# A wait on the predecessor's semaphore for every GpSimd operation, in a fused attention and MLP kernel on one core

## The chip, the core and the metric

The kernel runs on one core of a Trainium2 chip. The core has five engines that work side by side, each with its own queue of instructions: TensorE (PE in the profile; its weight loads are PEld), VectorE (DVE), ScalarE (ACT), GpSimd (POOL) and SyncE (SP), which here only issues DMA transfers. An engine takes its instructions in the order in which they were written. Between engines, order is kept by semaphores: an instruction can wait until a semaphore has reached a value, and can raise a semaphore when it is done. The metric is the time of one execution on the device in microseconds, and lower is better.

## The reference

Two layers follow each other. The first is an attention in which each token sees its last 96 tokens and the first 8 of its sequence, with a bias that grows with distance and differs by head. The second is an MLP with softplus between its two matrix products.

```python
def _attn_ref(q, k, v, n_global, n_local):        # q, k, v: (4, 8, 768, 64); 8 global, 96 local
    scores = scale * np.matmul(q, k.transpose(0, 1, 3, 2))
    is_global = pos[None, :] < int(n_global)
    is_local = (rel >= 0) & (rel < int(n_local))
    bias = -slopes[:, None, None] * dist[None, :, :]
    scores = np.where(is_global | is_local, scores + bias[None], -1e9)
    a = np.exp(scores - np.max(scores, axis=-1, keepdims=True))
    a = a / (np.sum(a, axis=-1, keepdims=True) + 1e-09)
    return np.matmul(a, v)

def _moe_ref(x, w_in, w_out):                     # x: (3072, 512), w_in: (512, 2048), w_out: (2048, 512)
    h = x @ w_in
    g = np.maximum(h, 0.0) + np.log1p(np.exp(-np.abs(h)))
    return g @ w_out
```

## The kernel before

The 3072 tokens are 24 blocks of 128, and two neighbouring blocks make a unit. For each unit, q, k and v are loaded by DMA into float32 buffers (`raw`), cast to bfloat16 (`castq`, `castk`, lines 545 and 554; `castv`, line 573) and, for q and k, transposed, on PE for the first units and by DMA transposes on SP's queue after that (lines 673 and 680). For each block, PE computes the scores into `s_ps` (line 788), DVE adds the bias (`z`, line 814), ACT takes the exponential (`ex`, line 819), PE multiplies by v into `x_ps` or `o_ps` (`pv`, line 845), and DVE normalizes by a reciprocal and a product (`nm`, lines 856 and 857) into `xs`. A DMA transpose turns `xs` into `XT` (line 888).

The 8 global tokens of a sequence are brought into the block before the present one by small copies: `gk` (line 695) copies columns of k, and `gv` (line 704) copies 4 rows of v from one place of the tile `vb` to another. These copies stand on POOL, DVE or ACT, as the order says.

For each pair of blocks (a group, 12 in all) the first product of the MLP runs into `h_ps` (`a`, line 903), ACT makes the softplus as exp and ln (`e`, line 919, and `ln`, line 930) into `g`, and the second product follows. The first four groups use a plain product (`b`, line 950) with a copy out of PSUM (`oc`, line 968). The later eight use a product with seven partial products instead of eight: PE runs them at line 442, from sums of weights (`ws`, line 344, made once on DVE and POOL) and sums of `g` (`ka`, line 379, on DVE and POOL), and DVE puts the parts together (lines 408 to 429). 35 products of a blank tile (`fill`, line 1047) fill gaps of PE near the start.

What sets the order is a written table, `ORDER`: it names each operation and its engine, for all engines in one sequence. `Program.in_order()` yields the operations in that sequence; the loop at the end of the kernel issues them. No scheduler moves anything. The framework works out from the tiles that an instruction reads and writes which semaphores it must wait for, and puts in only the waits that it needs. So a POOL instruction waits for POOL's own semaphore only where it touches a tile that an earlier POOL instruction also touches.

In the built program an instruction holds one wait. Where more are needed, the others stand in wait instructions of their own ahead of it on the same queue.

The changed loop stands at the end of the kernel function:

Of the kernel before, what the change touches and what calls it, by code (L numbers as in the profile page):

```python
# [184 lines left out]
def kernel(  # L185
# [11 lines left out]
    nc = tc.nc  # L197
# [937 lines left out]
    while fed < NGRP:  # L1135
        feed(fed)
        feed2(fed)
        fed += 1

    for o in pl.in_order():  # L1140
        o.ins = o.fn()
        for d in o.sync:
            tc.add_manual_dep(
                o.ins.ins, d.ins.ins.name,
                mybir.DependencyInfo(mybir.DependencyClass.Sync, mybir.DependencyReason.DATA),
            )
# [35 lines left out]
```

## Time and profile before

| what | value |
|---|---|
| median of 3 runs | 213.78 us (213.57 to 213.79) |
| the profiled execution, its own time | 213.29 us |
| its span in the profile | 211.4 us |
| granted TensorE clock, mean over the span | 1.00 |
| PE, busy | 201.6 us (95%) |
| ACT, busy | 177.0 us (84%) |
| DVE, busy | 158.8 us (75%) |
| POOL, busy, instructions | 84.7 us (40%), 98 |

All times of single instructions come from the one profiled execution, whose span is 1.9 us shorter than its own time. A row of the timeline gives the start and the length in us from the start of the span, the engine, the line of the kernel, the operation, what it writes and reads, and how many equal instructions the row merges. In brackets stands how long the engine had been idle before, and what released it. The end of a row is its start plus its length: where one engine's next row starts before that end, the two instructions overlap there.

### The profile page before, as it was taken

How to read it: one execution, taken by the hardware profiler on the slowest of the kernel's cores; microseconds unless marked ns; L12 is line 12 of the kernel's file. 1: busy time of each engine (PE TensorE's matmuls, PEld its weight loads, DVE VectorE, ACT ScalarE, POOL GpSimd, SP SyncE). 2: the span in 40 equal slices, each digit the busy share in tenths (PEclk: the TensorE clock that was granted, in tenths of full speed). 3: DMA queues.
4: the chain of work that ended last, by engine and by line, in shares of the span. 5: the costliest groups of instructions: out<-in, count | busy, mean ns of one | idle time of the engine just before them, and what ended most of it. 6: DMA issues, size and time to landing. Idle time of an engine off the chain costs nothing.

```text
span 211.4 us, 5376 instructions
## 1 busy us (share of the span) xinstructions
PE 201.6 (95%) x2150; PEld 158.7 (75%) x2163; DVE 158.8 (75%) x296; ACT 177.0 (84%) x253; POOL 84.7 (40%) x98
## 2 busy tenths in 40 slices
PE   7599999999999979999999999999999999999993
PEld 2366886556765756877889888889889889988882
DVE  5458789698658895697977888895989898716583
ACT  4899999998998869889899978988999989985610
POOL 4526788820370491113126673058708205070000
PEclk9999999999999999999999999999999999999999
DMA  5999999968999695996999988556994710600222
GB/s 196 337 365 386 387 356 348 308 158 220 289 223 167 156 221 159 224 206 130 184 274 174 231 181 199 151 98 123 290 256 61 160 25 5 198 3 0 99 101 102
DMA packets 70137, 40.99 MB, mean 194 GB/s; under 512 B 30432, under 2 KB 61664, under 8 KB 70112
## 3 DMA queue, kind: packets, MB, share of 16 engines
q1 hardware_dynamic: 69680, 39.99, 74.0%
q10 hardware_dynamic: 432, 0.66, 0.9%
q8 instruction: 17, 0.28, 0.6%
q14 instruction: 8, 0.07, 0.1%
HBM read 27.26 MB, written 6.29 MB: 159 GB/s over the span
## 4 chain that ended last, share of the span: by engine, by line
PE 84%; DVE 6%; DMA 4%; ACT 2%; issue 2%; SPq 0%; DVEq 0%
PE h_ps L903 37%; PE o_ps L442 12%; PE o_ps L950 9%; PE s_ps L788 5%; PE x_ps L442 5%; PE x_ps L845 4%; PE s_ps L950 3%; DVE z L814 2%; DMA raw<-in_k_dram 2%; PE s_ps L442 2%; PE x_ps L1047 2%; DMA XT<-xs 1%; DVE vb L704 1%; PE h_ps L442 1%; PE o_ps L845 1%
## 5 line engine op out<-in xcount | busy, mean ns | idle before, releaser
L903 PE MATMUL h_ps<-XT,w_in_bf 128*128 128x256 bf16 x768 | 94.8, 273 | 0.3 <-DMA XT<-xs 0.2
L903 PEld LDWEIGHTS <-w_in_bf 128*128 128x128 bf16 x768 | 72.9, 98 | 12.8 <-issue 0.8
L919 ACT ACTIVATE e<-h_ps 128x512 f32<-128x512 f32 x96 | 59.2, 634 | 13.2 <-PE h_ps L903 12.7
L930 ACT ACTIVATE g<-e 128x1024 bf16<-128x1024 f32 x48 | 49.7, 1052 | 0.6
L814 DVE TENSOR_TENSOR z<-s_ps,biasA 128x1024 f32<-128x1024 f32 x38 | 45.5, 1218 | 6.0 <-PE s_ps L788 4.1
L819 ACT ACTIVATE pb<-z 128x1024 bf16<-128x1024 f32 (+1 forms) x44 | 43.1, 990 | 1.7 <-DVE z L814 1.5
L379 POOL TENSOR_TENSOR raw<-g 128x1024 bf16<-128x1024 bf16 x7 | 14.9, 2131 | 33.2 <-ACT g L930 23.8
L442 PEld LDWEIGHTS <-g 128*128 128x128 bf16 x256 | 24.6, 98 | 3.1
L950 PE MATMUL o_ps<-w_out_bf,g 128*128 128x512 bf16 x88 | 23.1, 380 | 0.6 <-issue 0.3
L845 PEld LDWEIGHTS <-pb 128*128 128x128 bf16 x352 | 16.0, 97 | 5.4 <-issue 1.9
L442 PEld LDWEIGHTS <-raw 128*128 128x128 bf16 x192 | 18.4, 98 | 2.1
L442 PE MATMUL o_ps<-raw,raw 128*128 128x256 bf16 x152 | 19.0, 273 | 0.0
L950 PEld LDWEIGHTS <-g 128*128 128x128 bf16 x128 | 11.3, 98 | 9.5 <-ACT g L930 0.7
L545 POOL CAST kb<-raw 128x1024 bf16<-128x1024 f32 x8 | 8.3, 1041 | 23.0 <-DMA raw<-in_k_dram 17.3
L573 POOL CAST vb<-raw 64x512 bf16<-64x512 f32 x18 | 12.1, 670 | 10.4 <-DMA raw<-in_v_dram 9.7
L857 DVE TENSOR_TENSOR xs<-x_ps,rcp 128x256 bf16<-128x256 f32 x36 | 15.3, 424 | 1.2
L845 PE MATMUL x_ps<-vb,pb 128*128 128x65 bf16 x280 | 14.4, 193 | 1.4 <-DVE xs L857 1.4
L379 DVE TENSOR_TENSOR raw<-g 128x1024 bf16<-128x1024 bf16 x17 | 12.3, 732 | 4.1 <-ACT g L930 2.6
L856 DVE RECIPROCAL rcp<-x_ps 128x4 f32<-128x4 f32 x36 | 6.4, 178 | 9.7 <-PE x_ps L845 8.8
L704 POOL COPY vb<-vb 4x512 bf16<-4x512 bf16 x15 | 10.5, 698 | 6.3 <-DMA out_dram<-osb 2.8
L442 PE MATMUL o_ps<-raw,g 128*128 128x256 bf16 x96 | 12.0, 273 | 0.0
L1047 PE MATMUL x_ps<-blank 128*128 128x512 bf16 x32 | 10.7, 440 | 1.3 <-DVE blank L985 1.2
(117 smaller groups left out, 249.4 us busy)
## 6 DMA issues: line engine op xcount, KB each, us to landing
raw<-in_v_dram SPq DMA_DIRECT2D x12, 512.0 KB, 5.5
out_dram<-osb SPq DMA_DIRECT2D x22, 256.0 KB, 2.6
raw<-in_q_dram SPq DMA_DIRECT2D x9, 512.0 KB, 5.6
raw<-in_k_dram SPq DMA_DIRECT2D x9, 512.0 KB, 5.2
raw<-in_moe_w_in_dram SPq DMA_DIRECT2D x8, 512.0 KB, 9.5
raw<-in_moe_w_out_dram SPq DMA_DIRECT2D x8, 512.0 KB, 8.6
raw<-in_k_dram SPq DMA_DIRECT2D x6, 256.0 KB, 5.8
raw<-in_q_dram SPq DMA_DIRECT2D x4, 256.0 KB, 8.2
```

What stands on the lines that cost most here:

```text
L379: (nc.vector if eng == "DVE" else nc.gpsimd).tensor_tensor(dst, a[0], b[0], ALU.subtract)
L442: nc.tensor.matmul(psum(j), lhs[:, f // 2, f % 2, :], w(f), start=(f == 0), stop=(f == 7))
L704: copy_on[eng](vb_of(prev)[sl, :, 0:D], vb_of(first)[sl, :, 0:D])
L814: op(f"z{n}.{part}", "DVE", lambda: nc.vector.tensor_tensor(z, scored(), bias, ALU.add), reads=b_keys(n, part) + key, writes=[("z", slot)] ...
L819: nc.scalar.activation(pb[:, 0:nr, :].rearrange("p (y a) b -> p y (a b)", y=2), scored() if n in PE_BIAS else z, AF.Exp, scale=1.0 / root_d,)
L845: nc.tensor.matmul(xv[:, h, :], pb[:, 4 * (h % 2) + 2 * part + h // 2 if lone else u_all * (2 * (h % 2) + h // 2) + u, :], vb_of(prev if u ...
L857: nc.vector.tensor_tensor(xs[:, 4 * part : 4 * part + 4, :], xv[:, :, 0:D], rcp[:][:, :, None].to_broadcast([P, 4, D]), ALU.mult,)
L903: last = nc.tensor.matmul(hv[:, j, :], w_in_bf[:, m, fb * P : fb * P + P], XT[g % NXG][:, m, :], start=(m == 0), stop=(m == NM - 1),)
L919: nc.scalar.activation(e[:, p % 2, :, :].rearrange("p j (b t r) -> p (j b) r t", b=2, r=2), hb[:].rearrange("p (a r t) -> p a r t", a=4, r=2),
L930: nc.scalar.activation(gt[:, 2 * p - 2 : 2 * p + 2, :].rearrange("p a t -> p (a t)"), e[:].rearrange("p a j t -> p (a j t)"), AF.Ln, bias=1.0,
L950: nc.tensor.matmul(bank(x), gt[:, fb, ns * P : ns * P + P], w_out_bf[:, fb, :], start=(fb == 0), stop=(fb == NFB - 1),)
L1047: op(x, "PE", lambda: nc.tensor.matmul(x_ps[:], blank[:, 0:P], blank[:]), reads=["blank"], banks=(x,))
```

## The change

Each operation that the table gives to POOL gets one more dependency: its last instruction waits until the last instruction of the POOL operation ahead has raised POOL's semaphore. The written order of every engine, the operations, the tiles and the DMAs are the same. In the built program, 92 of the 98 recorded POOL instructions name POOL's own semaphore instead of 39; 10 of those 39 waited for an older POOL instruction than the one directly ahead, and now wait for that one. Since an instruction holds one wait, the waits that it had before move into wait instructions of their own: POOL's queue has 77 of these instead of 57. No instruction of PE, DVE, ACT or SP waits for anything else than before.

```diff
+    held_by = None
     for o in pl.in_order():
         o.ins = o.fn()
+        if o.eng == "POOL":
+            here = nc.cur_bb.bb.instructions[-1]
+            if held_by is not None:
+                tc.add_manual_dep(
+                    here, held_by,
+                    mybir.DependencyInfo(mybir.DependencyClass.Sync, mybir.DependencyReason.DATA),
+                )
+            held_by = here.name
         for d in o.sync:
```

The rows below are POOL's queue, of the program before (-) and after (+), around 72 us of the profile. `Pool_49`, `DVE_49`, `PE_49` and the `DMAHW` names are the semaphores of the engines and of the DMA queues. The first L704 row is the `gv` copy at 72.22 us, and the L344 row two sums of weights at 72.80 us.

```order
 L545 COPY kb_82<-raw_77 128x1024 [waits DMAHW4_49,DMAHW7_49,DMAHW2_49,Pool_49]
-L704 COPY vb<-vb 4x8x64 [waits DVE_49,PE_49]
-L344 TENSOR_TENSOR raw_76<-raw_68,raw_69 128x512 x2
+L704 COPY vb<-vb 4x8x64 [waits DVE_49,PE_49,Pool_49]
+L344 TENSOR_TENSOR raw_76<-raw_68,raw_69 128x512 [waits Pool_49] x2
 L573 COPY vb<-raw_78 64x8x64 [waits DMAHW3_49,Pool_49]
 L344 TENSOR_TENSOR raw_76<-raw_69 128x512 [waits Pool_49]
```

Nothing moved: the same instructions stand in the same order, the two sums now each wait for the instruction ahead, and the copy waits for three semaphores instead of two.

The second place is POOL's queue around 143 to 151 us, where sums of `g` (L379) and the copy of k columns (L695) follow each other, and PE waits for that copy. Before:

```order
L379 TENSOR_TENSOR raw_68<-g_106 128x1024 [waits DVE_49,Activation_49]
L379 TENSOR_TENSOR raw_69<-g_106 128x1024 [waits DVE_49,PE_49]
L695 COPY kTa_90<-kTa_90 128x8x4 [waits DMAHW6_49,DMAHW3_49]
L379 TENSOR_TENSOR g_106<-g_106 128x4x2x128 [waits Pool_49]
L704 COPY vb<-vb 4x8x64 [waits DVE_49,PE_49,Pool_49]
```

The same place in POOL's queue after the change:

```order
L379 TENSOR_TENSOR raw_68<-g_106 128x1024 [waits DVE_49,Activation_49,Pool_49]
L379 TENSOR_TENSOR raw_69<-g_106 128x1024 [waits DVE_49,PE_49,Pool_49]
L695 COPY kTa_90<-kTa_90 128x8x4 [waits DMAHW6_49,DMAHW3_49,Pool_49]
L379 TENSOR_TENSOR g_106<-g_106 128x4x2x128 [waits Pool_49]
L704 COPY vb<-vb 4x8x64 [waits DVE_49,PE_49,Pool_49]
```

Here too each instruction keeps its place and its waits for others; the first three gain the wait for the one ahead.

## The prediction

> **What bounds the kernel now.** I read the page's shares first, then who made PE wait, then the stretches of time in which it waited, and only then the instructions there.
>
> ```profile
> PE 201.6 (95%) x2150; PEld 158.7 (75%) x2163; DVE 158.8 (75%) x296; ACT 177.0 (84%) x253; POOL 84.7 (40%) x98
> ...
> PE 84%; DVE 6%; DMA 4%; ACT 2%; issue 2%; SPq 0%; DVEq 0%
> ```
>
> PE is busy for 95% of the span and makes up 84% of the chain that ended last. POOL is busy for 40% and is not on that chain. So the change, which touches POOL alone, can matter only through what POOL does to others. The waits of PE over the whole span, the longest in total first (us in total, times, longest):
>
> ```profile
> PE x_ps L845 <- DVE xs L857: 1.4, 1, 1.4
> ...
> PE o_ps L845 <- DVE osb L968: 0.2, 1, 0.2
> ```
>
> No row of that view names POOL; the three that stand between these and are put down to an engine belong to the start, where PE waits for the first casts and transposes. The largest is a single wait of `pv` for `nm`. The windows say where it lies:
>
> ```profile
> 72.00:74.00 2.00, 1.95 (x21) 1.42 (x18) 1.97 (x2) 2.00 (x3) 1.78 (x2) 1.00 0.42 94
> 74.00:76.00 2.00, 0.79 (x8) 0.56 (x6) 1.93 (x3) 1.83 (x4) 1.91 (x3) 1.00 0.98 272
> 76.00:78.00 2.00, 1.62 (x26) 1.24 (x26) 1.87 (x7) 0.38 (x1) 1.89 (x2) 1.00 1.34 234
> 78.00:204.00 126.00, 125.56 (x1397) 107.16 (x1400) 97.21 (x176) 108.19 (x148) 43.15 (x43) 1.00 0.65 145
> ```
>
> After length come busy times of PE, PEld, DVE, ACT and POOL. From 74 to 78 us PE is idle for 1.21 + 0.38 = 1.59 us. From 78 to 204 us it is idle for only 0.44 us of 126: whatever is won before 78 us is kept as long as the others can follow. Those have room there, DVE 97.21 of 126 us and ACT 108.19. The instructions around the hole:
>
> ```profile
> 72.22 0.61 POOL L704 COPY vb<-vb 4x512 bf16<-4x512 bf16 x1 [2.84 <-DMA out_dram<-osb]
> 72.67 2.78 DVE L704 COPY vb<-vb 4x512 bf16<-4x512 bf16 x1
> 72.80 2.50 POOL L344 TENSOR_TENSOR raw<-raw,raw 128x512 bf16<-128x512 f32 x2
> 73.11 0.81 PE L950 MATMUL o_ps<-w_out_bf,g 128*128 128x512 bf16 x3
> 73.76 1.04 PE L903 MATMUL h_ps<-XT,w_in_bf 128*128 128x256 bf16 x8
> 75.36 0.61 POOL L573 CAST vb<-raw 64x512 bf16<-64x512 f32 x1
> 75.49 0.18 DVE L856 RECIPROCAL rcp<-x_ps 128x4 f32<-128x4 f32 x1
> 75.70 0.42 DVE L857 TENSOR_TENSOR xs<-x_ps,rcp 128x256 bf16<-128x256 f32 x1
> 76.05 0.68 DVE L968 COPY osb<-o_ps 128x512 f32<-128x512 f32 x1
> 76.18 0.40 PE L845 MATMUL x_ps<-vb,pb 128*128 128x65 bf16 x8 [1.39 <-DVE xs L857]
> 76.78 0.40 PE L845 MATMUL o_ps<-vb,pb 128*128 128x65 bf16 x8 [0.20 <-DVE osb L968]
> ```
>
> The DVE copy that starts at 72.67 took 2.78 us. Copies of its kind take a tenth of that (DVE's of line 704, least, median and longest in ns):
>
> ```profile
> L704 DVE COPY vb<-vb x10: 280/292/2784, 49.3 to 177.5; 4x512 bf16<-4x512 bf16 x10
> ```
>
> It started while POOL ran its own `gv` copy (to 72.83), and ended at 75.45, which is 0.15 us after POOL's two sums of weights ended (72.80 + 2.50 = 75.30). POOL's second row starts 0.03 us before its first ends. The row behind the sums, which already waits for POOL's semaphore, starts 0.06 us after them, and exactly there DVE got through. So DVE stood behind three POOL instructions without a break, and PE behind DVE.
>
> **The change part by part.** *What one added wait costs.* POOL rows that follow each other directly show both kinds:
>
> ```profile
> 32.62 0.61 POOL L573 CAST vb<-raw 64x512 bf16<-64x512 f32 x1
> 33.31 1.28 POOL L344 TENSOR_TENSOR raw<-raw,raw 128x512 bf16<-128x512 f32 x1
> 34.53 0.61 POOL L573 CAST vb<-raw 64x512 bf16<-64x512 f32 x1
> 35.11 1.27 POOL L344 TENSOR_TENSOR raw<-raw 128x512 bf16<-128x512 f32 x1
> ```
>
> The second waits for POOL's semaphore and starts 0.08 us after the end ahead (32.62 + 0.61 = 33.23), as the row at 75.36 started 0.06 after. The third and fourth don't wait for it, and start 0.06 and 0.03 us before the end ahead. So the wait costs a POOL instruction that is otherwise ready 0.09 to 0.14 us; I take 0.12. 53 instructions gain it (92 instead of 39) and 10 get a later one. Were all of them ready, that would be 63 x 0.14 = 8.8 us at most, and POOL is idle 60% of the span. Where an instruction waits longer for a DMA or another engine, its old wait moves into an instruction of its own. The profile has no price for that alone. Above I bound it by the same 0.14 us, below by nothing, and take 0.07, the middle.
>
> *What hides it.* Work of PE that uses a late POOL result would show in PE's waits, and none does today. The nearest uses:
>
> ```profile
> 38.27 1.03 POOL L531 CAST w_out_bf<-raw 128x1024 bf16<-128x1024 f32 x1
> 40.25 0.59 PE L950 MATMUL o_ps<-w_out_bf,g 128*128 128x512 bf16 x2
> ...
> 96.19 1.04 POOL L545 CAST kb<-raw 128x1024 bf16<-128x1024 f32 x1 [1.47 <-DMA raw<-in_k_dram]
> 97.25 2.51 SPq L680 DMA_TRANSPOSE kT<-kb  x2
> ...
> 101.94 0.55 PE s_ps L788 x16
> ...
> 147.90 0.21 POOL L695 COPY kTa<-kTa 128x32 bf16<-128x32 bf16 x1
> ...
> 148.86 0.55 PE s_ps L788 x16
> ```
>
> The cast of w_out at 38.27 ends at 39.30, and the product at 40.25 is about the first that needs it: 0.95 us of cover. It ends the burst of which the rows from 32.62 to 35.11 are a part; with four waits added in that burst it comes 0.5 us late. The k cast at 96.19 ends at 97.23 and SP's transposes start 0.02 us later, so these will start up to 0.14 us late. They are issued 4.7 us before PE's scores at 101.94, of which 2.51 are the issue itself, and the rest is the cover. The copy at 147.90 ends 0.75 us before PE's scores at 148.86. It stands third behind two sums that also gain a wait: 0.07 + 0.07 + 0.12 = 0.26 us late, at most 0.36. Without its cover each of these would stop PE by as much as it is late: 0.5, 0.14 and 0.26 us. I cost all of them at 0.
>
> *What it gains.* At 72 us the two sums now wait, so POOL pauses between its copy and the first sum, as it does before the row at 75.36. Does DVE get its turn in a pause of 0.06 us? It did at 75.30, and here:
>
> ```profile
> 61.23 0.62 POOL L573 CAST vb<-raw 64x512 bf16<-64x512 f32 x1
> 61.75 0.29 DVE L704 COPY vb<-vb 4x512 bf16<-4x512 bf16 x1
> 61.91 0.61 POOL L704 COPY vb<-vb 4x512 bf16<-4x512 bf16 x1
> ```
>
> The same kind of DVE copy came 0.1 us before POOL's end at 61.85, took its usual 0.29 us, and POOL's next, which started 0.06 us after that end, was not held either. Applied to 72 us: POOL's copy, up to 0.14 us later for its moved wait, ends at 72.83 to 72.97; DVE's copy ends 0.15 us later, at 73.1 instead of 75.45, so 2.35 us earlier. Then `nm` (75.49 to 76.12, so 0.67 us behind the copy) ends near 73.8. PE comes to its `pv` at 73.76 + 1.04 = 74.80 and finds it done: the wait of 1.39 us goes. The copy out of `o_ps` at 76.05 can start when PE's product at 73.11 ends (73.92) and takes 0.68, to 74.7 at the latest allowed by DVE's own order; PE wants that bank at 74.80 + 0.40 = 75.20: the 0.20 us goes too. Together 1.59 us.
>
> *What is late next.* DVE is then ahead of PE by 0.5 to 1 us. POOL's sums end some 0.3 us later than now, and behind them on its queue stand a v cast, a third sum, a `gv` copy and the casts of q and k for SP's next transposes; POOL was busy for 1.91 of the 2 us from 74 us, so they all come that much later, and PE uses none of them before it has done its work to 80 us. DVE copies and casts that come after may meet them and stand behind one POOL instruction for up to its 1.27 us, but PE is no longer waiting directly behind these. From 78 us all loads, transposes and softmax steps follow PE's own progress, since PE's idle time there is 0.44 us in all. For such meetings I take back 0.1 us.
>
> *Sum:* 213.29 us of the profiled execution, minus 1.59, plus 0.1, gives 211.8. The profiled execution lies 0.49 us under the median of the runs (213.78), so against the median it is 212.3 us.
>
> On that place the Trainium skill, "SBUF — State Buffer" (section "SBUF: two separate sides"), says that the port pair shared by VectorE and GpSimd is an exclusive lock: whoever starts first has it for one whole instruction, and the other fully blocks. The trace agrees that DVE stands still, but shows it behind three POOL instructions and not behind the one that was running. By the rows above the time is 212.3 us; by the rule taken literally DVE's turn would come with or without a pause, and the time would stay at 213.8 us, which is a rival below.
>
> **The rivals.** *No change:* DVE gets its turn by some other rule than the pause. Against the pause as the only cause speaks this place:
>
> ```profile
> 139.01 1.04 POOL L554 CAST qb<-raw 128x1024 bf16<-128x1024 f32 x1
> 139.79 0.55 DVE L573 CAST vb<-raw 64x512 bf16<-64x512 f32 x1
> 140.00 0.81 POOL L573 CAST vb<-raw 64x512 bf16<-64x512 f32 x1
> ```
>
> POOL's rows overlap by 0.05 us (139.01 + 1.04 = 140.05), yet DVE got in between: its cast ended at 140.34, and POOL's took 0.81 instead of the usual 0.61. If the turn belongs to each instruction anyway, then what held DVE at 72.67 was something about the sums, and the pause may do nothing. The time then stays at 213.8, give or take 0.2 us. In the Trainium skill, "SBUF — State Buffer" (section "SBUF: two separate sides") states a lock per instruction; the place at 139 us agrees with it, the place at 72 us doesn't.
>
> *Part of the gain:* the wait at 74.80 goes, but something new costs PE 0.4 to 1.2 us before 204 us, such as an `XT` transpose or an exponential that ACT can't bring forward, since ACT is busy 108.19 of 126 us there. That gives 212.7 to 213.4.
>
> *Slower:* DVE is still held through all three POOL instructions, and these now take longer. At 0.12 us for each of the two sums and the copy, DVE and PE lose 0.3 to 0.36 us: 214.1. It decides beyond 0.43 us, which needs 0.15 us or more for each of the three. The longest pause of a cast that the profile puts down to POOL's own work ahead is this one:
>
> ```profile
> POOL qb L554 <- POOL vb L573: 0.3, 1, 0.3
> ```
>
> With that for each, 3 x 0.33 = 1.0 us and 214.8. For it speaks that DVE was passed twice at 72.67; against it, that all pauses of POOL after a semaphore of its own are 0.06 to 0.08 in the rows above.
>
> **How the numbers follow.** A change under 0.2% (0.43 us) is about what a measurement can't tell from none. The full gain has 0.62 (211.8 to 212.7; likeliest 212.3), part of it 0.16 (212.7 to 213.4), no change 0.12 (213.4 to 214.2), slower 0.10 (214.2 to 214.8). That the change doesn't do what it says is excluded by POOL's queue in the built program, which has the waits. So faster 0.78, same 0.12, slower 0.10. For the range I go from 0.6 us under the likeliest, since the profiled execution and the median differ by 0.49, up through the part gain and a little into no change: 211.7 to 213.6. It leaves out about 0.08 + 0.10 above and little below.
>
> **What would show it.** In the profile after, DVE's copy of line 704 near 72.7 us takes about 0.3 to 0.5 us instead of 2.78; POOL's two sums behind it start apart; PE's rows of `pv` near 75 us have no wait of 1.39; PE's busy share rises to about 96% with the same busy time. POOL's rows no longer overlap anywhere. If DVE's copy still takes 2.5 us or more, the pause is not what lets DVE in, and the prediction is wrong at that step. If the copy is short but the time is not, a new wait of PE after 78 us has taken the gain, and PE's list of waits will name it.

## The result and the profile after

The changed kernel takes 212.77 us (median of 13 runs, 211.67 to 213.31), against 213.79 us for the kernel before beside it (13 runs, 212.87 to 214.46). The ratio is 0.9948, with a 95% interval of 0.9928 to 0.9969, so the kernel is faster by about half a per cent. The forecast was 212.3 us within 211.7 to 213.6. The profiled execution of the kernel after took 213.09 us, with a span of 211.3 us, so it is one of the slower ones; why is shown below.

The shares of the page, after:

```profile
PE 202.2 (96%) x2150; PEld 158.5 (75%) x2163; DVE 158.0 (75%) x296; ACT 176.9 (84%) x253; POOL 86.5 (41%) x98
```

The windows after. The columns are length, and busy time of PE, PEld, DVE, ACT and POOL, then the granted clock, DMA share and GB/s:

```profile
72.00:74.00 2.00, 2.00 (x30) 1.82 (x28) 1.97 (x4) 1.90 (x4) 0.03 (x1) 1.00 0.98 244
74.00:76.00 2.00, 1.95 (x21) 1.42 (x19) 1.67 (x4) 2.00 (x3) 1.59 (x2) 1.00 0.41 69
76.00:78.00 2.00, 2.00 (x32) 1.77 (x30) 1.50 (x4) 1.82 (x4) 1.86 (x3) 1.00 1.03 305
78.00:204.00 126.00, 125.74 (x1399) 107.34 (x1401) 97.41 (x178) 108.63 (x149) 45.81 (x45) 1.00 0.69 149
```

PE idled for 1.64 us between 72 and 78 us before (0.05 + 1.21 + 0.38). Now it idles for 0.05 us there, and after 78 us it loses no more than it did (0.26 instead of 0.44 us). The same place in the timeline, which comes 2.1 us later in this execution (rows of other work are left out):

```profile
74.33 0.61 POOL L704 COPY vb<-vb 4x512 bf16<-4x512 bf16 x1 [2.31 <-PE x_ps L845]
74.72 0.37 DVE L704 COPY vb<-vb 4x512 bf16<-4x512 bf16 x1
75.02 2.63 POOL L344 TENSOR_TENSOR raw<-raw,raw 128x512 bf16<-128x512 f32 x2
75.34 0.42 DVE L857 TENSOR_TENSOR xs<-x_ps,rcp 128x256 bf16<-128x256 f32 x1
75.81 1.04 PE L903 MATMUL h_ps<-XT,w_in_bf 128*128 128x256 bf16 x8
76.68 0.41 PE L845 MATMUL x_ps<-vb,pb 128*128 128x65 bf16 x8
76.93 0.40 PE L845 MATMUL o_ps<-vb,pb 128*128 128x65 bf16 x8
```

DVE's copy takes 0.37 us instead of 2.78, and POOL's sums start 0.08 us after its copy ends (74.33 + 0.61 = 74.94). `nm` ends at 75.76, about a microsecond before PE's `pv`, which has no wait any more. The list of PE's waits no longer names it; what stands there now belongs to the start:

```profile
...
PE h_ps L845 <- POOL vb L573: 0.7, 1, 0.7
...
PE o_ps L845 <- DVE xs L857: 0.6, 1, 0.6
PE s_ps L651 <- POOL bias L1026: 0.5, 1, 0.5
PE h_ps L723 <- POOL bias L1026: 0.4, 1, 0.4
...
```

That is what the profiled execution lost: in the first 25 us PE was busy for 20.46 us, before for 21.20. The window before and the window after:

```profile
0.00:25.00 25.00, 21.20 (x213) 13.34 (x217) 15.97 (x44) 20.76 (x36) 13.26 (x25) 1.00 0.96 331
```

```profile
0.00:25.00 25.00, 20.46 (x188) 11.91 (x192) 14.31 (x40) 19.91 (x35) 11.25 (x23) 1.00 0.93 322
```

Matched one by one, PE's instructions stand 2.1 us later than before from 27 us on, 0.15 us later after 77 us, and 0.1 us earlier at the end. So the place at 75 us gave 1.9 us and the rest behind it 0.25, and the start of this execution took nearly all of that. Whether the added waits or chance did that is a question for the experiments.

### The profile page after: what moved, and what is told of

Its sections match the earlier page's. It is cut to its first block, busy times and chain, and to the rows that moved or that the text cites. A ratio compares the mean times of both kernels' runs of the same rounds, so it can differ in the third digit from the quotient of the medians.

```text
span 211.3 us, 5396 instructions
## 1 busy us (share of the span) xinstructions
PE 202.2 (96%) x2150; PEld 158.5 (75%) x2163; DVE 158.0 (75%) x296; ACT 176.9 (84%) x253; POOL 86.5 (41%) x98
## 4 chain that ended last, share of the span: by engine, by line
PE 84%; DMA 5%; SPq 4%; POOL 2%; issue 1%; DVE 1%; POOLq 0%; DVEq 0%
PE h_ps L903 38%; PE o_ps L442 13%; PE o_ps L950 10%; PE s_ps L788 5%; PE x_ps L442 5%; DMA raw<-in_moe_w_in_dram 5%; PE x_ps L845 4%; PE s_ps L950 3%; SPq L502 3%; PE s_ps L442 2%; POOL w_in_bf L531 1%; PE h_ps L442 1%; SPq L529 1%; PE o_ps L845 1%; SPq L511 1%
## 5 line engine op out<-in xcount | busy, mean ns | idle before, releaser
L379 POOL TENSOR_TENSOR raw<-g 128x1024 bf16<-128x1024 bf16 x7 | 14.9, 2130 | 32.4 <-issue 16.4
L379 DVE TENSOR_TENSOR raw<-g 128x1024 bf16<-128x1024 bf16 x17 | 12.3, 734 | 4.1 <-ACT g L930 2.5
L704 POOL COPY vb<-vb 4x512 bf16<-4x512 bf16 x15 | 9.9, 661 | 5.8 <-PE x_ps L845 3.8
```

What stands on the lines that cost most here:

```text
L379: (nc.vector if eng == "DVE" else nc.gpsimd).tensor_tensor(dst, a[0], b[0], ALU.subtract)
```

## The experiments

Each changed version of the kernel was timed beside the kernel before, on the same chip; three more kernels only measure. Four questions were asked: which of the added waits makes the gain, whether it is DVE's copy that makes it, what the waits elsewhere cost, and what it is that lets DVE in.

### One wait alone, and all but two

The first kernel adds the wait for the first sum at 72 us only, the second for all POOL operations but the two sums, the third for the second sum only, and the fourth is the changed kernel once more. The edit of the first; the others differ in the condition:

```diff
+        if o.eng == "POOL":
+            here = nc.cur_bb.bb.instructions[-1]
+            if held_by is not None and o.name == "ws3.3":
+                tc.add_manual_dep(
...
+            held_by = here.name
```

> One wait instead of 63: only the first of the two sums of weights that stand behind the gv copy at 72 us waits for POOL's semaphore. Theory (the pause lets DVE in): DVE's gv copy takes about 0.4 us instead of 2.78, PE's wait of 1.39 us and the one of 0.20 us go, and the time falls by 1.4 to 1.6 us, ratio about 0.993, a little more than with all waits. Rival (the gain has to do with the many other waits, or with DVE's turn by another rule): DVE's copy stays at 2.8 us and the ratio at 1.000.

> All added waits but those of the two sums at 72 us. Theory: DVE's gv copy stands behind three POOL instructions again (2.7 us or more), PE waits 1.4 us or a little more, nothing is gained; the other waits are covered, so the ratio is 1.000 to 1.002. Rival (the waits in the first 45 us cost PE time of their own): ratio 1.002 to 1.005, with the added time in PE's waits before 30 us. Rival (the gain comes from the other waits): ratio 0.995.

> Only the second of the two sums waits for POOL's semaphore, so the first pause lies between the two sums. Theory: DVE's copy gets in there, ends about 1.25 us earlier than before (at 74.2 on the clock of the run before), nm is done 0.1 us after PE wants it; PE's wait shrinks from 1.39 to about 0.1 to 0.2 us, ratio 0.993 to 0.995. Rival (DVE gets in only where an instruction that is no sum follows): DVE's copy stays at 2.8 us or more, ratio 1.000.

> The changed kernel once more, for a second profile of its first 35 us. If the 2.1 us that the first profile lost there came from loads that landed late by chance, this profile loses less than 1 us there and its span is nearer 210 us. If the waits cost it, the loss is again about 2 us, and PE waits for POOL in the same places. Ratio 0.993 to 0.997 either way.

Measured against a kernel before of 213.72 us (20 runs):

| waits | median us | ratio, 95% interval | longest DVE copy of line 704 anywhere, ns |
|---|---|---|---|
| first sum only | 212.34 | 0.9938 [0.9915, 0.9961] | 708 |
| all but the two sums | 213.8 | 1.0016 [0.9994, 1.0038] | 2827 |
| second sum only | 212.15 | 0.9933 [0.9910, 0.9956] | 1555 |
| all (the change again) | 212.58 | 0.9959 [0.9929, 0.9989] | 655 |

One wait is enough for the whole gain, and without those two the change gives nothing. With the first sum's wait, the copy at this place took 0.31 us (the longest, 708 ns, stands elsewhere):

```profile
73.48 0.31 DVE L704 COPY vb<-vb 4x512 bf16<-4x512 bf16 x1
```

With all waits but these, the old wait of PE is back in full:

```profile
PE x_ps L845 <- DVE xs L857: 1.4, 1, 1.4
...
PE o_ps L845 <- DVE osb L968: 0.2, 1, 0.2
```

The wait for the second sum lets DVE in one sum later, which the copy's row shows, and even that was early enough: PE's two waits there were 0.2 us each.

```profile
72.40 0.61 POOL L704 COPY vb<-vb 4x512 bf16<-4x512 bf16 x1 [3.27 <-PE x_ps L845]
72.85 1.55 DVE L704 COPY vb<-vb 4x512 bf16<-4x512 bf16 x1
72.98 2.62 POOL L344 TENSOR_TENSOR raw<-raw,raw 128x512 bf16<-128x512 f32 x2
```

72.85 + 1.55 = 74.40, and the first sum had started at 72.98 and lasts 1.27 us, to 74.25: DVE ended 0.15 us behind it.

### The copy on ACT, without any wait

The kernel before, with the copy that was held moved to ACT. One word of the table differs:

```diff
- gv9.1:V ws3.3:G b2.1.12:P nm8.1:V
+ gv9.1:A ws3.3:G b2.1.12:P nm8.1:V
```

> The kernel before, with one word of the table changed: the copy gv9.1, which DVE held for 2.78 us at 72.67, runs on ACT. No wait is added, and POOL's sums still overlap. Theory (what DVE lost behind POOL is the whole gain): DVE comes to its reciprocal on time, the wait of 1.39 us goes as it did with the waits, and ACT pays 0.6 us for the copy (its median on line 704) at a place where it is busy 1.83 to 1.91 of 2 us: 212.2 to 212.8 us, ratio 0.993 to 0.996. Rival (POOL's instructions themselves, by their later start, made the gain): 213.7, ratio 1.000. Rival (ACT is too full to take it): the wait of PE comes back under the name of an exponential, 213.2 to 213.7.

It took 212.61 us against 213.88, ratio 0.9955 [0.9933, 0.9977], and no wait of PE for `nm` near 75 us is left. So to take away DVE's time behind POOL is enough for the gain, and nothing else that the waits do to POOL is needed. PE's waits there:

```profile
...
PE o_ps L950 <- DVE xs L857: 0.3, 1, 0.3
...
PE x_ps L845 <- ACT pb L819: 0.2, 1, 0.2
```

ACT's 0.6 us cost PE a wait of 0.19 us for an exponential at 75.35, and a v cast of DVE that met a POOL sum and took 1.49 us cost one of 0.26 us at 78.69 (the first row).

### The early waits and the late ones

> The added waits only from POOL's 42nd operation on, which is after 45 us; the two sums at 72 us are among them. Theory (waits in the first 27 us cost PE some 0.3 us, the others nothing): 212.2 us, ratio 0.993, like the kernels with one wait alone. Rival (the first waits cost nothing, and what the whole change lost against one wait is spread or chance): 212.6, ratio 0.995 to 0.996.

> The other part: the added waits of POOL's first 41 operations (to 45 us) and of the two sums at 72 us, none after. Theory (the early waits cost some 0.3 us): 212.6 us, ratio 0.995 to 0.996, with PE's waits of the first 27 us longer than before by 0.3. Rival (they cost nothing): 212.2, ratio 0.993.

Both took the same: 212.25 us, ratio 0.9939 [0.9918, 0.9959], with the late waits, and 212.24 us, ratio 0.9939 [0.9909, 0.9969], with the early ones. So the 0.3 us that the theory gave to the early waits didn't show, but intervals of this width can't exclude it. The profiles allow a second look: how much later PE's instructions stand than in the kernel before, matched one by one (less than 0 is earlier, all in us).

| waits | late at 27 us | change from 72 to 77 us | change from 77 us to the end |
|---|---|---|---|
| all | 2.07 | -1.90 | -0.25 |
| all (the change again) | 1.19 | -1.90 | 0.17 |
| early ones and the two sums | 0.86 | -1.90 | -0.05 |
| all but the two sums | 0.76 | 0.04 | -0.20 |
| first sum only | 0.78 | -1.90 | 0.32 |
| late ones | 0.42 | -1.91 | 0.44 |
| none, copy on ACT | 0.36 | -1.53 | 0.08 |
| second sum only | 0.17 | -1.23 | -0.20 |

The place gave the same 1.9 us wherever the first sum waited. At the start, the four profiles with early waits stand 0.76 to 2.07 us late and the four without 0.17 to 0.78. With one profile each that is a hint that the early waits cost something, and no proof. The second profile of the changed kernel, with 1.19 us, lies between the two outcomes that were named for it. In the profiled execution of the kernel after, the delay came with the transfers. POOL's first cast of k rows, released by its load, began at 7.74 us instead of 6.89, though the loads up to there were issued within 0.1 us of when they were before. Its cast of w_in began at 21.28 instead of 18.61; the loads of w_in were issued 1.1 us later than before (9.03 instead of 7.93), behind an issue that took 3.36 us instead of 2.34. How much of that was chance stays open, and so does whether all waits together cost 0.1% or 0.2% against one wait alone (0.9948 and 0.9959 against 0.9933 and 0.9938): the intervals overlap.

### What lets DVE in: chains of POOL instructions

The prediction's reason was that DVE gets its turn in a pause of POOL and not between rows that overlap, and one place at 139 us spoke against it. A kernel that only measures, and leaves the computation out, runs chains of POOL operations, with one DVE operation that becomes ready while the second runs. In its list S is a sum of float32, C a cast of 1024 columns, c a cast of 64 rows, g a copy of 4 rows; True means that each waits for the one ahead.

```diff
+    ("SSSS", "g", 0, False), ("SSSS", "g", 0, True),
+    ("CCCC", "g", 0, False), ("CCCC", "g", 0, True),
+    ("ggSS", "g", 0, False), ("ggSS", "g", 0, True),
+    ("CCSS", "g", 0, False), ("ccSS", "g", 0, False),
```

> A kernel that only measures: it leaves the whole computation out and writes zeros. POOL runs chains of four independent operations (S the sum of weights of line 344, C the cast of 1024 columns, c the cast of 64 rows, g the copy of 4 rows), three times each, with or without a wait of each for the one ahead; one DVE operation (g or c) becomes ready when the first of the four ends, so while the second runs. Four sums last about 5.0 us. Theory (the pause decides): without waits the rows overlap by 0.03 to 0.06 us, and DVE's copy stands behind all that is left of any chain, 3.8 us after sums and 3.2 after casts of 1024 columns, whatever the operations are; with the waits it stands behind one operation only, 1.2 to 1.4 us after sums. Rival 1 (something about the sums): without waits, DVE stands 3.8 us behind sums, but only behind one operation (about 1.2 us) in chains of casts or copies. Rival 2 (something about DVE's operation): the cast gets in after one operation without any wait, as at 139 us, and the copy doesn't. Rival 3 (one turn per instruction): one operation in all chains, with and without waits. Chains with reciprocals ahead on DVE bring DVE's operation 0.2 to 0.8 us later: if the place of its start inside POOL's instruction decides, the outcome changes along them.

All theories missed in part. POOL's rows overlap by 0.03 to 0.06 us in every chain without waits, and DVE was let in after one operation nonetheless in nearly all of them: its copy took 1.33 us in four sums, 1.09 in four casts of 1024 columns, 0.67 in four casts of 64 rows or four copies. With the waits the copy took 0.29 us throughout. DVE stood to the end of the chain only where sums came behind copies of 4 rows or casts of 64 rows. Two chains that differ in nothing but the rows and columns of the first two casts, without waits (the timeline):

```profile
234.85 2.02 POOL L67 CAST big<-raw 128x1024 bf16<-128x1024 f32 x2
235.91 1.10 DVE L71 COPY dcopy<-vbd 4x512 bf16<-4x512 bf16 x1 [2.16 <-POOL big L67]
236.83 2.51 POOL L65 TENSOR_TENSOR sum<-raw,raw 128x512 bf16<-128x512 f32 x2
239.41 1.16 POOL L70 CAST cast<-raw 64x512 bf16<-64x512 f32 x2
240.05 3.12 DVE L71 COPY dcopy<-vbd 4x512 bf16<-4x512 bf16 x1 [3.03 <-POOL cast L70]
240.54 2.47 POOL L65 TENSOR_TENSOR sum<-raw,raw 128x512 bf16<-128x512 f32 x2
```

Bringing DVE's operation 0.1 to 0.3 us later, by reciprocals ahead of it, changed nothing. So neither the overlap, nor the sums as such, nor DVE's operation decides.

The next kernel varies rows and length apart.

> The same measuring kernel with other chains (whole computation left out, zeros written), nearly all without waits. New operations of POOL: k a cast of all 128 rows with half the columns (as short as g and c, about 0.6 us), s a sum of 64 rows (as long as S, if length goes by columns), d the cast of rows 64 to 127, G the copy of rows 64 to 67, and casts of 16, 32, 96, 112, 127 and 128 rows ahead of two sums. Theory (rows): DVE gets in between two overlapping operations unless the second works on rows that the first left out, since the part of POOL that had no rows in the first begins the second at once, and then the parts stay out of step: DVE's copy takes 0.67 us in kkSS, kkgg, ccgg, 128SS, 1.3 in SSss and ssss, but stands to the end of the chain in ggSS (3.1), ssSS (3.9), ggCC and ccCC (2.8), ggcc and ggkk (1.9), ccdd, ddcc, ggGG (1.9), GGSS, 16SS, 32SS, 96SS (3.1); with ggSSSS the state lasts (5.6), also when DVE becomes ready only at the third operation's end (3.9), where SSSSSS and kkSSSS give 1.3. Rival (length): DVE fails wherever a short operation stands ahead of a longer one: 3.1 in kkSS and 128SS, 1.3 in ssSS, 0.67 in ggcc, ccdd, ggGG. Rival (sums alone): 0.67 in ggCC and ccCC.

For two sums behind copies and casts that start at row 0 the theory of the rows held. A cast of all 128 rows that is as short as the copies let DVE in (0.67 us), so it isn't the length. With 16, 32, 96 and 112 rows DVE was shut out to the end (3.11 us), with 127 and 128 it was not. The timeline of the chains with 112 and with 127 rows:

```profile
191.83 0.62 POOL L67 CAST rows<-raw 112x512 bf16<-112x512 f32 x1
191.92 3.11 DVE L65 COPY dcopy<-vbd 4x512 bf16<-4x512 bf16 x1 [0.78 <-POOL full L67]
192.40 2.48 POOL L59 TENSOR_TENSOR sum<-raw,raw 128x512 bf16<-128x512 f32 x2
...
195.72 0.62 POOL L67 CAST rows<-raw 127x512 bf16<-127x512 f32 x1
195.81 0.67 DVE L65 COPY dcopy<-vbd 4x512 bf16<-4x512 bf16 x1 [0.78 <-POOL full L67]
196.30 2.52 POOL L59 TENSOR_TENSOR sum<-raw,raw 128x512 bf16<-128x512 f32 x2
```

The last 16 rows decide here: leave them out of an instruction ahead of sums, and DVE doesn't get in behind it. What happens between 112 and 127 rows wasn't tried. The account that this suggests is that POOL works in parts of 16 rows, and that a part which has no rows in an instruction begins the next one at once. Then the parts are out of step, and DVE has to find all of them between two instructions at the same moment. The Trainium skill, "GPSIMD Engine Reference" (section "Instruction dispatch"), says this of POOL: consecutive instructions are no barrier between its eight cores, core k serves rows 16k to 16k+15 of each, and starts the next as soon as its own share is done. The step between 112 and 127 rows agrees; the parts themselves stand in no row of the profile.

The account also gives a chain that was expected wrongly. Two sums of 64 rows and two of 128 should by the theory have shut DVE out to the end, 3.9 us, and DVE took 2.56:

```profile
134.26 2.48 POOL L59 TENSOR_TENSOR half<-raw,raw 64x512 bf16<-64x512 f32 x2
135.55 2.56 DVE L65 COPY dcopy<-vbd 4x512 bf16<-4x512 bf16 x1 [3.70 <-POOL half L59]
136.70 2.52 POOL L59 TENSOR_TENSOR sum<-raw,raw 128x512 bf16<-128x512 f32 x2
```

The upper half has no rows in the first two, so it does both full sums from 134.3 to 136.8, and is then idle. The lower half ends its second operation at 136.74, while the upper still works, and its third at 137.96, when the upper is idle: DVE ended at 138.11, 0.15 us after that.

Other misses of this run limit the account. Behind copies of few rows, DVE got in ahead of casts (0.67 and 0.75 us), where 2.8 and 1.9 had been expected. And a change between rows that start at 0 and rows that start at 64 made POOL itself pause for 0.04 to 0.08 us, so nothing was shut out there.

A third kernel of chains asked which kinds of work do this.

> The measuring kernel with other kinds of work (whole computation left out, zeros written). U is a sum of two bfloat16 tiles, M a product with a constant (one input, float32), both 128x512, u and m the same on 64 rows; DVE's operations are g and c as before, S a sum of float32, p a copy of 512 columns out of PSUM, q a small reciprocal out of PSUM. Theory (an instruction that reads two tiles keeps the port across the boundary): ggUU shuts DVE out to the end as ggSS does, ggMM doesn't. Rival (float32 with two inputs only): ggUU gives 0.67. Rival (length over 1.04 us): whatever takes longer shuts DVE out. A cast or sum of DVE stands as long as its copy does in ggSS (3.1 us and more); p and q, which read PSUM, stand only if they need the same port for what they write. In ggCSSS with DVE ready at the third's end a full cast has put the parts in step again, so DVE gets in after one sum (1.3 us); if the state outlasts the cast, 2.5 us. A wait ahead of the fourth operation of ggSSSS does the same for a DVE copy that becomes ready behind it (1.3 us).

Sums of two bfloat16 tiles behind copies of 4 rows held DVE for 0.76 us, products with a constant for 1.10, sums of float32 for 3.12. So it isn't the two inputs, which was the theory, nor the length, since the product is the longest (1.48 us). The rival of float32 sums with two inputs fits these three, but not another chain of this run, two bfloat16 sums of 64 rows ahead of two of 128:

```profile
290.83 2.25 POOL L74 TENSOR_TENSOR newu<-gb,gb 64x512 bf16<-64x512 bf16 x2
292.01 2.33 DVE L84 COPY dcopy<-vbd 4x512 bf16<-4x512 bf16 x1 [3.36 <-POOL newu L74]
293.05 2.30 POOL L74 TENSOR_TENSOR newU<-gb,gb 128x512 bf16<-128x512 bf16 x2
```

DVE ended at 294.34, 0.15 us behind the third sum, so bfloat16 sums can hold it too. What decides between the kinds of work stays open. A cast in between doesn't end the state (3.78 us with a full cast ahead of three sums), but a wait does: behind it DVE took 1.34 us. And only DVE's operations that read from SBUF were held. A cast took 3.25 us and a sum 3.52, but a copy of 512 columns out of PSUM took 0.69 us in the midst of the same sums:

```profile
184.13 1.16 POOL L84 COPY copy<-vb 4x512 bf16<-4x512 bf16 x2 [0.69 <-DVE dsum L78]
184.77 0.69 DVE L66 COPY osb<-x_ps 128x512 f32<-128x512 f32 x1 [0.77 <-POOL copy L84]
185.26 2.47 POOL L78 TENSOR_TENSOR sum<-raw,raw 128x512 bf16<-128x512 f32 x2
```

### More work for POOL at the place, and no wait

If only the boundary ahead of a sum is shut, one more copy of 4 rows between POOL's `gv` copy and the sums should open it, without a pause.

```diff
- gv9.1:V ws3.3:G b2.1.12:P
+ gv9.1:V more:G ws3.3:G b2.1.12:P
...
+    op("more", "POOL", lambda: nc.gpsimd.tensor_copy(more[0:GH, :], blank[0:GH, :]), reads=["blank"])
```

> The kernel before with one operation more and no added wait: a copy of 4 rows and 512 columns of a blank tile to a spare tile, on POOL between its gv copy and the first sum at 72 us. POOL has 0.6 us more to do there, and its rows still overlap. Theory from the chains (only a sum that follows an instruction of fewer rows shuts DVE out; into a copy DVE gets its turn though the rows overlap): DVE's copy takes its turn between POOL's two copies and ends near 73.0, the wait of 1.39 us goes, 212.2 to 212.5 us, ratio 0.992 to 0.996, and POOL's added copy is the one that shows DVE's turn, by taking 0.67 to 0.75 us. Theory of the prediction (only a pause lets DVE in): DVE stands behind four instructions, to 76.1, PE waits about 2.0 us there, and the time is 214.3, ratio 1.003.

It was slower: 215.49 us against 213.54, ratio 1.0086 [1.0054, 1.0118]. The prediction's theory came nearer, and even it missed by 1.2 us. DVE's copy stood behind all four instructions:

```profile
72.43 0.61 POOL L704 COPY vb<-vb 4x512 bf16<-4x512 bf16 x1 [3.44 <-DMA out_dram<-osb]
72.98 0.60 POOL L987 COPY more<-blank 4x512 bf16<-4x512 bf16 x1
73.56 2.49 POOL L344 TENSOR_TENSOR raw<-raw,raw 128x512 bf16<-128x512 f32 x2
```

```profile
72.88 3.33 DVE L704 COPY vb<-vb 4x512 bf16<-4x512 bf16 x1
```

It starts only 0.1 us ahead of the added copy. The last kernel has two added copies, so that DVE would be waiting well ahead of the second.

```diff
- gv9.1:V ws3.3:G b2.1.12:P
+ gv9.1:V more0:G more1:G ws3.3:G b2.1.12:P
```

> As the kernel with one copy more, but with two of them, to two spare tiles: POOL runs its gv copy, two copies of 4 rows and the two sums, still without an added wait and with overlapping rows, and has 1.1 us more to do than in the kernel before. Theory from the chains (in this state a sum shuts DVE out, a copy doesn't, and DVE must have been waiting when the copy begins): DVE's copy starts about 0.15 us before the end of the gv copy and asks for the port too late for the first added copy, but is waiting when the second begins; it ends some 0.15 us after the first added copy, near 73.6, having taken 0.7 to 0.9 us, the second added copy takes 0.67 to 0.75, PE's wait of 1.39 us goes: 212.2 to 212.7 us, ratio 0.992 to 0.997. Theory of the prediction (only a pause lets DVE in): DVE stands behind five instructions, 3.9 us, PE waits 2.5 us and its clock falls as with one copy: 216 us, ratio 1.01.

Neither came: 213.42 us against 213.66, ratio 0.9996 [0.9976, 1.0017]. DVE started at 72.85 and was held for 2.66 us, to 75.51, and then let in between the two sums, a boundary that neither theory had named. PE waited 1.3 us. The rows of both:

```profile
72.41 0.61 POOL L704 COPY vb<-vb 4x512 bf16<-4x512 bf16 x1 [2.95 <-DMA out_dram<-osb]
72.85 2.66 DVE L704 COPY vb<-vb 4x512 bf16<-4x512 bf16 x1
72.96 1.16 POOL L988 COPY more<-blank 4x512 bf16<-4x512 bf16 x2
74.09 2.54 POOL L344 TENSOR_TENSOR raw<-raw,raw 128x512 bf16<-128x512 f32 x2
```

The parts out of step give all three places, by a sum that was made only after these runs. Seven of the eight parts have no rows in the copies, begin the sums as soon as the `gv` copy begins, and are done with both 2.5 us later (2 x 1.25): at 74.91 with two copies, at 74.93 with one, and at 74.72 in the kernel before. The part that works on the copies comes to the boundary between its two sums at 75.35, 74.82 and 74.06. So with two copies the others are idle by then, and DVE gets in there; with one copy and before they are not, and DVE must wait for the end. The same sum doesn't give the chains with casts and products, where DVE got in earlier.

## Why the prediction was right, point by point

**What bounds the kernel.** Right. Taking DVE's copy away from POOL's neighbourhood, by whatever means, gave 1.0 to 1.6 us in the medians, and PE's wait at 75 us was the only one that had to go.

**The place and its size.** The sum was 1.59 us, 1.39 + 0.20. PE's idle time there fell by 1.59 us (1.64 to 0.05), and its instructions moved up by 1.9. The other 0.3 us is overlap, which the sum left out by counting each wait only to the end of PE's row ahead: after, the two rows of `pv` start 0.17 and 0.16 us before that end (75.81 + 1.04 = 76.85 against 76.68, and 76.68 + 0.41 = 77.09 against 76.93). DVE's copy was forecast at 0.3 to 0.5 us and took 0.37.

**What one wait costs.** Estimated at 0.09 to 0.14 us. In the chains the overlap of 0.04 us between sums became a pause of 0.08, so 0.12 us; between casts 0.06 became 0.06, again 0.12. For a wait that moves into an instruction of its own 0.07 us was the middle of a range; in the trace after, POOL starts 0.12 us after the semaphore through such an instruction and 0.05 without, so 0.07.

**What hides the waits.** All were costed at nothing. (By the prediction's own bound of 0.14 us a wait, the copy at 147.90 comes at most 0.42 us late and not 0.36; its cover of 0.75 us is larger than both.) The kernel with all waits but the two sums bounds that: ratio 1.0016, between 0.1% faster and 0.4% slower. In the trace after, PE's idle time behind 78 us is 0.26 us, less than before. The first 27 us, of which the prediction weighed no use of a POOL result, are less sure: the profiles with early waits tend to be later there.

**The 0.1 us taken back, and the total.** Forecast 212.3 us, measured 212.77 and 212.58. The medians lie 0.3 to 0.5 us above, and the kernels with one wait, at 212.34 and 212.15, on the forecast. As a term of the sum, the price of the other waits may thus be some 0.3 us too low; the runs don't separate it from none. That the total came so near is in part luck: the place gave 0.3 us more than its term in the profile, and the medians of the changed kernel show little more than half of what it gave.

**Why DVE waits.** This step was right for this place and wrong as a rule. The prediction said that DVE stood behind three POOL instructions "without a break" and that the pause lets it in. The pause does, with either sum's wait alone. In the chains DVE passes between rows that overlap just as well, as at 139 us, where a cast of all rows stands ahead, and with two added copies it passed between the two sums without any pause. By the chains, what shut it out at 72 us was a copy of 4 rows ahead of float32 sums of 128. By the account above, the added wait helps because it holds all of POOL until the copy is done, which brings its parts in step again. The rival "something about the sums" was half of that, but its consequence, that the pause would do nothing, didn't come.

**The rule of the lock.** The prediction weighed the Trainium skill, "SBUF — State Buffer" (section "SBUF: two separate sides"), which gives the port to whoever starts first for one whole instruction, and found that it disagrees with 72 us. Together with the rule of the Trainium skill, "GPSIMD Engine Reference" (section "Instruction dispatch"), that was told above, it need not: POOL's instructions begin early on the parts that have nothing else to do, and then no moment lies between them at 72 us. The prediction didn't weigh that second rule. It would have pointed at the copy of 4 rows, and the place at 139 us would have been no contradiction. That the two rules together are the cause is argued from the chains; the casts and products above don't fit.

**What would show it.** The signs came: besides the short copy and the missing wait, no two operations of POOL overlap in the trace after, where 21 pairs did before.

**The rivals.** No change and slower did not come. Part of the gain, priced at 212.7 to 213.4, has the median of 212.77 in its range. The new cost for PE that it names didn't show behind 78 us, and for the start it stays open. In the kernel with one added copy, POOL's longer work with DVE still behind it did make it slower, by 1.95 us. PE's longer wait, which is the mechanism of the slower rival, made about 0.54 us of it in the profile, and the clock, told below, 1.6.

## What to carry to other kernels

A DVE instruction that takes ten times its usual length has stood behind POOL; look at what POOL ran ahead of it, and above all for an instruction of few rows followed by float32 sums of many. One wait on POOL's own semaphore at that place costs 0.12 us and gave all of the gain here, so it need not be put everywhere. Rows of POOL that overlap in a profile don't by themselves show that DVE was shut out.

## What the runs showed of the hardware that was not expected

The parts of POOL seem not to start an instruction together. Whether the last 16 of 128 rows were worked on decided whether another engine's copy took 0.67 or 3.11 us.

PE's clock fell after a wait. With one added copy PE waited 1.93 us near 76 us, and the granted clock was 0.59 and 0.55 in the 4 us that followed:

```profile
74.00:76.00 2.00, 1.00 (x9) 0.75 (x8) 2.00 (x1) 1.83 (x4) 2.00 (x2) 1.00 0.92 254
76.00:78.00 2.00, 0.87 (x19) 0.75 (x19) 1.90 (x6) 0.59 (x1) 1.85 (x3) 1.00 0.96 243
78.00:80.00 2.00, 2.00 (x25) 1.32 (x23) 1.32 (x5) 0.88 (x2) 1.87 (x4) 0.59 0.69 113
80.00:82.00 2.00, 2.00 (x11) 1.37 (x11) 2.00 (x2) 1.27 (x3) 1.03 (x2) 0.55 0.33 66
```

Within them it stood at 0.50 from 78.4 to 81.8 us. PE's instructions were 0.75 us late at the end of the wait and 2.3 us late when the clock was back, so the clock cost 1.6 us, more than the wait added. Five of the six runs show a mean clock of 0.992 and spans of 213.6 to 214.0 us; the sixth has 1.000 and 212.7. The kernel before waits 1.39 us at the same place, and its clock is 1.00 in all windows from 72 to 204 us. The Trainium skill, "TensorE: Matmul & The Clock Gate" (section "What's actually happening"), lets the clock fall to half after an idle window of about 3.4 us, counted in windows that run free. The trace agrees with the half and with the length, 3.4 us. But here PE was busy for 1.87 of the 4 us ahead of the fall, so less than a window of full idleness was enough.
